# Scores of a second-half attention head issued as one run over three PSUM banks, and half of the weight splits placed later

## The chip, the cores and the metric

The kernel runs on one core of one Trainium2 chip. The metric is the device time of one execution in microseconds (us), of which the median over several runs is taken. The engines are named as in the profile: PE does matmuls (PEld is its weight load), DVE, ACT and POOL are the three engines for elementwise work, and SP issues the DMAs.

## The reference, cut to what matters

Attention with a causal mask and a decay, over 4 batches, 8 heads, 576 positions and 64 columns, is followed by a mixture of four experts over all 2304 tokens:

```python
scores = scale * q @ k.T                      # scale = 1/8
cum    = cumsum(log(clip(f, 1e-4, 1)))
scores = where(causal, -1e9, scores + cum[:, None] - cum[None, :])
attn   = exp(scores - max(scores)); attn /= sum(attn) + 1e-9
x      = attn @ v                             # heads side by side: 2304 x 512
p      = domain_probs / (sum(domain_probs) + 1e-9)
out    = sum over e of p[:, e] * (relu(x @ w1[e]) @ w2[e])   # 512 -> 1024 -> 512
```

## The kernel before, in words

**Attention.** The 576 queries of a batch are cut into a first half (queries 0 to 255) and a second half (256 to 575). A job is a batch, a pair of heads and a half, and its two heads are worked off one after the other, so there are 64 heads in `heads`: 0 to 31 of the first half, 32 to 63 of the second. This document names them by that number. A second-half head has three query tiles, t = 2, 3 and 4, with 384, 512 and 576 keys. For each tile PE makes the scores by pairs of matmuls (`s<-hi` and `s<-kl,q` in the profile, line 615): the first with the high parts of q and k, the second with the low parts and the decays. DVE adds the mask and takes the row minimum (`qk_min`, line 629), ACT takes the exponential and its sum (`qk_exp`, line 644). When a head's three tiles are through, `recip16` and `turn16` split the scaled probabilities in two f16 parts (ACT line 713, DVE line 714) and SP transposes them by DMA (`pt<-z`, line 723). `av_pair` (line 816) multiplies the transposed probabilities of both heads of a job with v, in 28 matmuls, and `out16` (line 870) writes the result into x.

**Inputs of the scores.** `prep_hi` and `prep_lo` make the operands of a head: ACT casts `hi<-raw` (line 562), POOL casts `q<-raw` (line 563) and takes two differences (`kl`, line 571, and `hi`, line 577). There are two buffers for `raw` and `hi` and one `q2` tile for each of the two heads of a job, so those of head n + 2 wait until the scores of head n have been made. The probabilities `p` have six buffers, three for a head.

**Banks.** Scores, transposes, `av_pair` and the small products of `power` take banks from the pool `ps_a`, which has four. `qk_pe` takes a new bank whenever a piece doesn't fit in the last one. A tile with 576 keys is made as two pieces of 288, and called tile by tile (`qk_tile`) the four pieces of a head take four banks: one each for t = 2 and 3, two for t = 4.

**Experts.** A `Step` is one pair of weight units (256 of the 1024 hidden columns of an expert) for one chunk of 256 tokens: `l1` (24 matmuls, line 1012), `gate` (ACT line 1025 makes `gh`, DVE line 1026 makes `gl`), `l2` (12 matmuls, line 1045), and after every second one DVE adds to `acc` (line 1072). There are 80 steps in two sweeps. Sweep 0 takes steps 0 to 27. In sweep 1 (steps 28 to 79) a group of four units is used for 4, 3 or 2 chunks, so for 8, 6 or 4 steps, alternating between its first pair (ps = 0) and its second (ps = 1). The last four chunks (`LAST`) are done by 16 larger products afterwards (`Big`, line 1283, from about 625 us).

**Weights.** `w_split(n)` splits unit n into two f16 parts by three engines: ACT lines 979 and 974, DVE line 980, POOL lines 971 and 975. It also has SP load up to three further units (`w_load`, line 937; three buffers) and two steps later write the split unit to DRAM (line 988). After the last step of a pair (`ends`) the pair six units further on is split. As the two pairs of a group end in neighbouring steps, four units are split in two neighbouring steps.

**The order.** Outside `startup` the program order is a priority, and the framework's scheduler puts each engine's instructions in order by that priority and by its own estimate of when their inputs are ready. The program order comes from a list: `head_steps` gives every piece of a head with a cost, and `pace(n)` emits, between the quarters of step n, as many pieces as the costs allow at an even slope between goals. A goal is that the x of a chunk is complete three steps before the step which first uses it. For chunk 4 that is step 40. When the x of chunk c is complete, three pieces find its scale (`turn`: L260, L199, L202 to L252) and `narrow(c)` makes `y` from it (ACT line 475, DVE line 476), which line 1012 reads. `narrow` is asked for once at the start of each step.

## Time and profile before

| | us |
|---|---|
| median of 3 runs | 942.64 |
| lowest and highest | 941.62, 944.03 |
| the profiled execution | 939.25 |
| its span, first to last instruction | 937.5 |

| stretch of the profiled execution, us | what runs there |
|---|---|
| 0 to 245 | first-half heads, steps 0 to 27 |
| 245 to 357 | second-half heads 33 to 44, steps 28 to 39 |
| 357 to 600 | heads 45 to 63, steps 40 to 75 |
| 600 to 937.5 | last steps, then the larger products |

The profile is one execution, 3.4 us under the median. The first view to read is the busy time by stretch with the granted clock of PE (1.00 is 2.4 GHz, and the lower of the two levels is 0.5), then what PE waited for in a stretch, then the timeline of the stretch. A line of the timeline gives start, duration, engine, source line, operation, output and inputs, and in brackets how long the engine had been idle and what ended that.

### The profile page before, as it was taken

The page shows a single profiled execution, that of the slowest core. Times are in us where ns is not written, and L with a number is a line of the kernel's source. Part 1 is how long each engine was busy: PE and PEld are TensorE (multiplying, and loading weights), DVE is VectorE, ACT ScalarE, POOL GpSimd, SP SyncE. Part 2 cuts the span into 40 slices and gives each one's busy share as a digit, 9 for nine tenths or more (in the row PEclk, how much of TensorE's full clock was granted, in tenths as well). Part 3 has the DMA queues.
Part 4 walks back from the last instruction along what each step waited for, and adds up shares of the span by engine and source line. Part 5 has one row for each costly group of instructions (what it writes and reads, how often), then busy time and mean ns, then how long its engine had stood idle before and what let it go on. Part 6 is the DMA issues. An engine that isn't in the chain of part 4 may idle for free. (4 is left out here: it accounts for less than half of the span.)

```text
span 937.5 us, 16657 instructions
## 1 busy us (share of the span) xinstructions
PE 885.3 (94%) x5783; PEld 620.8 (66%) x5783; DVE 709.3 (76%) x1458; ACT 568.9 (61%) x1137; POOL 525.1 (56%) x528
## 2 busy tenths in 40 slices
PE   4899998999998889999999989999998999999998
PEld 3699988999765556666666656654455664666547
DVE  5768665786888988789878887576778757786487
ACT  5869755465676778668666777355665345653350
POOL 4657865478533754327641684265778627785060
PEclk9999999999998988999999999999999999999999
DMA  7458844538879698988999699524322424232003
GB/s 264 146 176 295 291 126 164 186 119 313 227 189 198 152 293 195 311 156 212 306 288 158 119 328 236 135 67 142 129 91 81 145 68 125 79 107 74 23 1 91
DMA packets 147508, 159.45 MB, mean 170 GB/s; under 512 B 86148, under 2 KB 107328, under 8 KB 147424
## 3 DMA queue, kind: packets, MB, share of 16 engines
q1 hardware_dynamic: 147424, 158.39, 60.2%
q8 instruction: 45, 0.74, 0.3%
q14 instruction: 39, 0.32, 0.2%
HBM read 117.30 MB, written 21.65 MB: 148 GB/s over the span
## 5 line engine op out<-in xcount | busy, mean ns | idle before, releaser
L1012 PE MATMUL l<-y,w 128*128 128x256 f16 x1248 | 155.7, 275 | 0.0
L1012 PEld LDWEIGHTS <-w 128*128 128x128 f16 x1248 | 118.3, 99 | 30.6 <-issue 6.5
L644 ACT ACTIVATE p<-p,nm 128x576 f32<-128x576 f32 (+3 forms) x160 | 95.6, 598 | 52.4 <-DVE nm L629 43.5
L1045 PE MATMUL l<-w,gh 128*128 128x512 f16 x408 | 122.6, 383 | 4.8 <-DVE acc L1072 4.8
L714 DVE SCALAR_TENSOR_TENSOR z<-p,rs,z 128x384 f16<-128x384 f32 (+3 forms) x128 | 85.7, 694 | 12.6 <-ACT z L713 11.1
L1072 DVE SCALAR_TENSOR_TENSOR acc<-y,scg,acc 128x256 f32<-128x256 f32 (+1 forms) x164 | 81.1, 515 | 14.9 <-PE y L1283 14.7
L615 PE MATMUL s<-hi 128*128 128x384 f32 (+1 forms) x192 | 76.9, 406 | 16.1 <-DVE hi L577 8.9
L563 POOL CAST q<-raw 64x320 fp32r<-64x320 f32 (+1 forms) x56 | 26.0, 465 | 117.9 <-PE s L615 71.3
L1283 PE MATMUL m<-rh,bs 128*128 128x512 f16 x256 | 86.4, 379 | 0.0
L629 DVE CUSTOM_DVE_ANT_0 p<-s,mask 128x288 f32<-128x288 f32 (+2 forms) x160 | 74.8, 475 | 12.9 <-PE s L615 11.8
L571 POOL TENSOR_TENSOR kl<-raw,hi 64x576 fp32r<-64x576 f32 (+1 forms) x56 | 66.4, 1186 | 28.6 <-ACT hi L562 28.2
L1045 PE MATMUL l<-w,gl 128*128 128x512 f16 x204 | 77.1, 383 | 5.0 <-DVE gl L1026 5.0
L1209 POOL TENSOR_TENSOR bs<-wt,bs 128x512 f16<-128x512 f32 x32 | 38.4, 1201 | 75.7 <-ACT bs L1208 75.4
L971 POOL TENSOR_SCALAR wr<-wr,wsc 128x512 f32<-128x512 f32 x32 | 53.9, 1687 | 35.1 <-DMA wr<-in_w 25.5
L956 POOL TENSOR_TENSOR wl<-wr,wh 128x512 fp32r<-128x512 f32 x48 | 64.4, 1370 | 15.9 <-ACT wh L952 11.6
L713 ACT ACTIVATE z<-p,rs 128x384 f16<-128x384 f32 (+3 forms) x128 | 69.5, 589 | 4.6 <-issue 1.2
L1026 DVE SCALAR_TENSOR_TENSOR gl<-l,gh 128x512 f16<-128x512 f32 (+1 forms) x80 | 54.7, 684 | 19.1 <-ACT gh L1025 18.6
L1012 PE MATMUL l<-xh,wh 128*128 128x256 f32 x224 | 65.0, 292 | 0.8 <-ACT xh L857 0.8
L615 PE MATMUL s<-kl,q 66*128 66x384 f32 (+1 forms) x192 | 63.7, 336 | 2.2 <-DMA kl<-nc 2.2
L1283 PE MATMUL m<-rh,bw 128*128 128x512 f16 x191 | 64.4, 379 | 1.4 <-ACT r L1329 1.4
L1012 PE MATMUL l<-xl,wh 128*128 128x256 f32 x224 | 65.2, 291 | 0.0
L1045 PEld LDWEIGHTS <-gh 128*128 128x128 f16 x408 | 37.0, 98 | 42.2 <-issue 11.2
(387 smaller groups left out, 2359.6 us busy)
## 6 DMA issues: line engine op xcount, KB each, us to landing
wr<-in_w SPq DMA_DIRECT2D x90, 512.0 KB
pk<-in_w SPq DMA_DIRECT2D x64, 256.0 KB
wd<-w SPq DMA_DIRECT2D x32, 512.0 KB
raw<-in_qk SPq DMA_DIRECT2D x32, 448.0 KB
bw<-wd SPq DMA_DIRECT2D x32, 256.0 KB
bv<-wd SPq DMA_DIRECT2D x32, 256.0 KB
raw<-in_qk SPq DMA_DIRECT2D x24, 256.0 KB
vp<-in_v SPq DMA_DIRECT2D x10, 512.0 KB
```

Of the source, the lines that this page charges most:

```text
L571: eng.tensor_tensor(out=kl[:64, :wk], in0=r[:64, ko : ko + wk], in1=hi[:64, ko : ko + wk].bitcast(F32), op=ALU.subtract,)
L615: nc.tensor.matmul(out=ps[:, at : at + z - a], lhsT=lhsT, rhs=rhs, start=(m == 0), stop=(m == 1),)
L629: nc.vector.tensor_tensor_reduce(out=pt[:, a:z], in0=ps, in1=mask[:, m0 + a : m0 + z], scale=-0.125, scalar=BIG if n == 0 else nm[:, col : ...
L644: nc.scalar.activation(out=pt[:, :w_], in_=pt[:, :w_], func=AF.Exp, scale=-1.0, bias=self.nmax[hh][:, c : c + 1], accum_out=self.ssum[:, h ...
L713: nc.scalar.activation(out=o[:, 0], in_=x, func=AF.Copy, scale=sc)
L714: nc.vector.scalar_tensor_tensor(out=o[:, 1], in0=x, scalar=sc, in1=o[:, 0], op0=ALU.mult, op1=ALU.subtract)
L956: eng.tensor_tensor(out=wl[n][:, a:z], in0=r[:, a:z], in1=wh[n][:, a:z].bitcast(F32), op=ALU.subtract,)
L1012: nc.tensor.matmul(out=self.l1p[:, fi, :], lhsT=lhsT, rhs=rhs[:, k, :], start=(k == 0 and m == 0), stop=(k == 3 and m == 2),)
L1026: self.last = nc.vector.scalar_tensor_tensor(out=self.gl, in0=self.l1p, scalar=0.0, in1=self.gh.bitcast(F32) if wide else self.gh, op0=ALU ...
L1045: matmul(out=l2[tt], lhsT=lhsT, rhs=rhs, start=(self.ps == 0 and fi == 0 and m == 0), stop=(self.ps == 1 and fi == 1 and m == 2),)
L1072: nc.vector.scalar_tensor_tensor(out=acc[c][:, tt, d0:d1], in0=ps, scalar=sc, in1=acc[c][:, tt, d0:d1], op0=ALU.mult, op1=ALU.add,)
L1283: line.append(nc.tensor.matmul(**args))
```

## The change

`qk_head` makes all scores of a second-half head in one call, over three banks taken together. Tile 2 lies in 384 columns of the first bank and tile 3 fills the second. Tile 4 is cut at key 448 instead of 288: its last 128 keys go into the 128 free columns of the first bank, its first 448 into the third. `qk_pe` loses the cut, since only first-half heads still call it. In the list, `qk_head` stands first with cost 1400, and then each tile's `qk_min` and `qk_exp` with cost 224. The sum is that of the three old costs (584 + 712 + 776 = 2072). `av_pair` of the job before, when there is one, stands after the third entry instead of the second, so after `qk_min` and `qk_exp` of tile 3.

`REST` postpones those calls of `w_split` that follow the end of a group's second pair, by 1, 2 or 3 steps where the group is used for 2, 3 or 4 chunks.

```diff
+REST = (0, 0, 1, 2, 3)
...
+        def qk_bank(self, hh, t):
+            return ps_a.tile([128, 512], F32, tag="a", name=f"s{self.nm}_{hh}_{t}")
+
+        def qk_piece(self, hh, t, a, z, ps):
+
+            o, i = self.qo + TOK0[t] - self.q0, TOK0[t] - self.q0
+            for m, (lhsT, rhs) in enumerate(
+                (
+                    (self.hi[hh][:, o : o + 128], self.hi[hh][:, self.ko + a : self.ko + z]),
+                    (q2[hh][:, i : i + 128], self.kl[hh][:66, a:z]),
+                )
+            ):
+                nc.tensor.matmul(out=ps, lhsT=lhsT, rhs=rhs, start=(m == 0), stop=(m == 1))
+            self.sp.setdefault((hh, t), []).append((a, z, ps))
...
-                cuts = ((0, w_),) if w_ <= 512 else ((0, w_ // 2), (w_ // 2, w_))
...
+                if at + w_ > 512:
+                    ps, at = self.qk_bank(hh, t), 0
+                self.qk_piece(hh, t, 0, w_, ps[:, at : at + w_])
+                at += w_
+
+        def qk_head(self, hh):
+
+            two, three, four = (self.qk_bank(hh, t) for t in (2, 3, 4))
+            self.qk_piece(hh, 2, 0, 384, two[:, :384])
+            self.qk_piece(hh, 4, 448, 576, two[:, 384:])
+            self.qk_piece(hh, 3, 0, 512, three)
+            self.qk_piece(hh, 4, 0, 448, four[:, :448])
...
+            if j.half:
+                qs.append((1400, lambda j=j, hh=hh: j.qk_head(hh)))
             for t in j.its:
-                qs.append((TOK0[t] + 328, lambda j=j, hh=hh, t=t: j.qk_tile(hh, t)))
+                if j.half:
+                    qs.append((224, lambda j=j, hh=hh, t=t: (j.qk_min(hh, t), j.qk_exp(hh, t))))
+                else:
+                    qs.append((TOK0[t] + 328, lambda j=j, hh=hh, t=t: j.qk_tile(hh, t)))
...
-            qs[2:2] = [(1000, j.av_pair), (0, j.out16)] + ready(n - 2)
+            qs[3:3] = [(1000, j.av_pair), (0, j.out16)] + ready(n - 2)
...
-                        w_split(w0 + 6)
-                        w_split(w0 + 7)
+                        wait = REST[len(SWEEPS[t.s][t.g // 2])] if t.ps else 0
+                        splits.setdefault(n + wait, []).extend((w0 + 6, w0 + 7))
                     first_units(w0)
+            for m in splits.pop(n, ()):
+                w_split(m)
```

## Rows read from the trace of the kernel before

**Rows 1.** The page: PE's busy time, and all row minima (count, busy, mean).

```profile
PE 885.3 (94%) x5783; PEld 620.8 (66%) x5783; DVE 709.3 (76%) x1458; ACT 568.9 (61%) x1137; POOL 525.1 (56%) x528
...
L629 DVE CUSTOM_DVE_ANT_0 p<-s,mask 128x288 f32<-128x288 f32 (+2 forms) x160 | 74.8, 475 | 12.9 <-PE s L615 11.8
```

**Rows 2.** By stretch: PE, PEld, DVE, ACT, POOL busy (count); PEclk; DMA share; GB/s.

```profile
245.00:357.00 112.00, 99.18 (x651) 66.11 (x650) 98.76 (x231) 78.46 (x159) 56.50 (x54) 0.90 0.89 217
357.00:600.00 243.00, 236.36 (x1761) 161.98 (x1758) 198.34 (x432) 165.97 (x336) 114.14 (x104) 1.00 0.92 225
```

**Rows 3.** What PE waited for, 245 to 357: total, times, longest.

```profile
PE s L615 <- POOL hi L577: 4.8, 2, 2.5
PE o L816 <- DMA pt<-z: 4.0, 1, 4.0
PE l L1045 <- DVE acc L1072: 2.5, 2, 1.9
PE l L1045 <- DVE gl L1026: 1.4, 2, 1.0
```

**Rows 4.** The timeline of PE around the scores of head 37.

```profile
288.89 0.44 PE L816 MATMUL o<-pt,v 128*64 128x320 f16 x1 [3.98 <-DMA pt<-z]
...
292.44 2.35 PE L816 MATMUL o<-pt,v 128*64 128x320 f16 x27
294.72 0.40 PE L615 MATMUL s<-hi 128*128 128x288 f32 x1
```

**Rows 5.** The timelines of DVE, ACT and POOL at the same place.

```profile
291.03 0.46 DVE L629 CUSTOM_DVE_ANT_0 p<-s,mask 128x288 f32<-128x288 f32 x1 [1.06 <-PE s L615]
...
295.30 0.52 DVE L629 CUSTOM_DVE_ANT_0 p<-s,mask,nm 128x288 f32<-128x288 f32 x1 [2.15 <-PE s L615]
...
296.12 0.94 ACT L562 ACTIVATE hi<-raw 128x896 fp32r<-128x896 f32 x1
...
295.39 0.45 POOL L563 CAST q<-raw 64x320 fp32r<-64x320 f32 x1 [10.17 <-DMA raw<-in_qk]
```

**Rows 6.** What DVE waited for, 245 to 357, the first line.

```profile
DVE p L629 <- PE s L615: 3.6, 4, 2.1
```

**Rows 7.** The timeline: `av_pair` of head 39, `y` of chunk 4, first matmul of step 40.

```profile
332.63 1.72 PE L816 MATMUL o<-pt,v 128*64 128x320 f16 x27
...
350.93 1.98 DVE L476 SCALAR_TENSOR_TENSOR y<-xf,xsc,y 128x1024 f16<-128x1024 f32 x1 [0.64 <-ACT y L475]
...
356.42 0.39 PE L1012 MATMUL l<-y,w 128*128 128x256 f16 x1
```

**Rows 8.** The timeline of PE: starts of score matmuls of 128, 288 and 512 columns.

```profile
221.40 0.28 PE L615 MATMUL s<-hi 128*128 128x128 f32 x1
221.51 0.28 PE L615 MATMUL s<-kl,q 66*128 66x128 f32 x1
...
302.06 0.40 PE L615 MATMUL s<-hi 128*128 128x512 f32 x1
302.30 0.40 PE L615 MATMUL s<-kl,q 66*128 66x512 f32 x1
...
423.75 0.29 PE L615 MATMUL s<-hi 128*128 128x288 f32 x1
423.88 0.30 PE L615 MATMUL s<-kl,q 66*128 66x288 f32 x1
```

**Rows 9.** What PE waited for, 357 to 600: total, times, longest.

```profile
PE l L1045 <- DVE gl L1026: 3.6, 3, 2.1
PE l L1045 <- DVE acc L1072: 1.7, 2, 1.3
PE o L816 <- DMA pt<-z: 1.3, 2, 1.0
```

**Rows 10.** The timeline: a split that waits for its raw unit, and PE after it.

```profile
541.22 0.72 ACT L979 ACTIVATE w<-wr,wsc 128x512 f16<-128x512 f32 x1 [4.58 <-DMA wr<-in_w]
...
543.44 0.59 PE L1045 MATMUL l<-w,gh 128*128 128x512 f16 x2 [1.32 <-DVE acc L1072]
```

More of the change, by code (lines that the diff above doesn't have):

```diff
@@ L600, in qk_pe @@
             for t in its:
-                o = self.qo + TOK0[t] - self.q0
                 w_ = TOK0[t] + 128
-                cuts = ((0, w_),) if w_ <= 512 else ((0, w_ // 2), (w_ // 2, w_))
-                for n, (a, z) in enumerate(cuts):
-                    if at + z - a > 512:
-                        ps = ps_a.tile([128, 512], F32, tag="a", name=f"s{self.nm}_{hh}_{t}_{n}")
-                        at = 0
-                    i = TOK0[t] - self.q0
-                    for m, (lhsT, rhs) in enumerate(
-                        (
-                            (self.hi[hh][:, o : o + 128], self.hi[hh][:, self.ko + a : self.ko + z]),
-                            (q2[hh][:, i : i + 128], self.kl[hh][:66, a:z]),
-                        )
-                    ):
-                        nc.tensor.matmul(
-                            out=ps[:, at : at + z - a],
-                            lhsT=lhsT,
-                            rhs=rhs,
-                            start=(m == 0),
-                            stop=(m == 1),
-                        )
-                    self.sp.setdefault((hh, t), []).append((a, z, ps[:, at : at + z - a]))
-                    at += z - a
+                if at + w_ > 512:
[8 more added lines that the diff above has]
+            self.qk_piece(hh, 4, 0, 448, four[:, :448])
         def qk_min(self, hh, t):
@@ L1618, in fused @@
         w_split(n)
-    used = set()
+    used, splits = set(), {}
     for n in range(len(steps) + 1):
```

## The prediction

> **What bounds the kernel now.** The page comes first: PE is busy for 885.3 of 937.5 us [rows 1], so at most the idle remainder and what a lower clock costs can be won without removing matmuls. The change removes none. The view by stretch shows where the remainder lies that the change can reach, since second-half heads run from 235 to 600 us only. From 357 to 600 us PE is busy for 236.4 of 243.0 us at full clock, which leaves 6.6 us. From 245 to 357 us it is busy for 99.2 of 112.0 us, and its mean granted clock is 0.90 [rows 2]. With levels of 1.0 and 0.5, a mean of 0.90 says that a fifth of the stretch, some 22 us, ran at the lower level, and half of that, 11 us, is time that the same matmuls would not have taken at the upper one. So this stretch holds 12.8 us of idle time and up to 11 us of slow matmuls, and it is the one to understand.
>
> Its end is not set by PE. Step 40 is the first to use chunk 4. The `av_pair` that completes this chunk's x (head 39) runs at 332.6 us, the last part of `y` is written from 350.9 to 352.9 us, and step 40 begins at 356.4 us [rows 7]. Step 39 had begun before 340, so PE had only attention left to do, and waited twice for its operands (4.8 us for POOL's `hi`, [rows 3]). The chain to this `y` runs through heads 33 to 39, whose work on DVE queues behind each other: DVE is busy for 98.8 of 112.0 us [rows 2]. So the stretch can shorten only by as much as DVE's 13.2 us of idle time allow.
>
> One place shows how the idle time arises. Behind tile 3 of head 37 stands, on PE, the `av_pair` of head 35, which waits 4.0 us for its transposes, until 288.9; the rest of it runs at 292.4, and the last two pieces of head 37 come at about 290 and at 294.7 [rows 4]. DVE, which needs them for its minima, sits idle for 1.06 and 2.15 us [rows 5], and these two are 3.2 of the 3.6 us that it waits for scores in the whole stretch [rows 6]. ACT's `hi` for head 39, which needs the buffer of head 37, comes at 296.1, directly after. Its raw data came hardly sooner, as POOL's cast of the same head waited for them until 295.4 [rows 5], so the buffer was not the only thing it lacked. Head 39 is the one that completes chunk 4.
>
> **The change part by part.**
>
> *Place of the scores.* I worked out the planner's positions by hand from the costs. Head 37 had tiles 2 and 3 at steps 29.25 and 29.75, `av_pair` of head 35 at 30.375, and tile 4 at 30.875. Now all scores stand at 29.625, the minima at 29.75 and 29.875, `av_pair` at 30.5, and the minimum of tile 4 at 30.625. Twelve heads lie in the stretch and all odd ones have this pattern. No score then stands behind an `av_pair` of the same section, so the 3.6 us of DVE waits go. `hi` and `q` of head n + 2 get their buffers earlier, and the `av_pair` stands half a step further from the `turn16` it needs (for head 37: 30.625 to 33.75 instead of 30.875 to 33.5), which is some 3 us (steps 40 to 75 take 243 us [rows 2], 6.7 us a step with the attention in it). DVE's idle time is what the chain to `y` can use, so I credit the 3.6 us to the end of the stretch. After `y` was ready, PE needed until 356.4, 3.5 us, for attention matmuls at the lower clock [rows 2, 7]. When there are fewer stalls ahead of it, part of this goes too: I take 2.0 us. Together −5.6 us. The bounds are 0 (DVE fills its idle time with something else) and −13.2 us (all of it is used).
>
> *Minima in one place.* The cost of the four minima of a head does not change: 0.475 us each [rows 1], 1.9 us a head, 128 + 448 columns being as many as 288 + 288. But three entries now stand 0.125 step apart, so up to 1.9 us of DVE work come together where single ones (at most two pieces) came before. Queued behind it on DVE are `gl`, which `l2` of PE waits for, and `acc`. In the stretch that PE sets (357 to 600, 19 heads) there are three stalls on `gl` of 1.2 us on average [rows 9]. I add one more, +1.2 us. The bounds are 0 and seven more, +8.4 us.
>
> *Pieces of 128 and 448.* Matmuls of 288 columns start 0.13 us apart, those of 512 columns 0.24, and those of 128 columns 0.11 [rows 8]. By the line between 288 and 512, one of 448 takes 0.21. A head had 4 × 0.13 = 0.52 for tile 4 and gets 2 × 0.11 + 2 × 0.21 = 0.64. That is +0.12 us a head, paid where PE is the bound: 19 × 0.12 = +2.3 us. The bounds are 0, if the short ones stream in proportion to their columns (0.06 us), and +3.7 us for 31 heads.
> The Trainium skill, "TensorE: Matmul & The Clock Gate", section "Back-to-back issue gap", speaks against this cut as well: it gives about 81 ns for a sustained matmul of 128 columns, well above the 56 ns of an isolated one, as the weight load has to fit in. By its figures the two cuts differ by an estimated 0.05 us a head, or 1 us in place of 2.3; the row is above the Trainium skill's figure.
>
> *Three banks at once.* The pool has four. A run needs three free ones, which are those of the head before after its last minimum, and `av_pair` takes the fourth. I cost this at nothing: PE's list of waits has no wait for `nm`, the minimum that frees a bank, in either stretch [rows 3, 9]. If that cover goes, while `power` holds a bank for chunk 4, the scores of head 42 wait for it, which is attention ahead of its need.
>
> *Chunk 4's scale.* The pieces of `turn` move from step 36.75 to 37.0, and `narrow` is therefore asked for at step 38 instead of 37. I cost this at nothing, as the chain runs 18 us behind its x by data (334.3 to 352.9), not by its place in the program [rows 7]. If it were set by place, it would cost the quarter step to one step, 1.7 to 6.7 us.
>
> *Splits.* The pairs that move are units 24, 28 and 32, 36, 44, 48, 52, 56 and 60 with their neighbours, by 1 to 3 steps. With each go its two casts on ACT, one instruction on DVE, two on POOL, and on SP the loads of the units behind it and two writes to DRAM, which then stand behind the transposes of later heads. The three raw buffers are what makes the fourth unit of a burst wait: ACT stands 4.6 us for a raw unit, and PE then waits 1.3 us for the `acc` queued behind on DVE [rows 10]. With two units at a time the raw data are there, −1.3 us; the bounds are 0 and −1.7 us, all waits for `acc` there [rows 9]. In the other direction, a pair that was split early may now fall into the tight stretch. It brings two instructions to DVE and four to ACT, and the later place of units 36 and 37 (28.99 to 30.99) lies in it. I take nothing for it, as it is far from the step that needs them.
>
> *Transposes later on.* The extra half step should also end the waits for `pt<-z` after 357: −1.3 us [rows 9], between 0 and that.
>
> **Sum.** −5.6 + 1.2 + 2.3 − 1.3 − 1.3 = −4.7 us. The profiled execution took 939.25 us, its span and 1.75 us around it, and would take 934.5. The median of the runs shown lies 3.4 us above the profiled execution; the same difference from the median of 942.64 gives 937.9 us, 0.5% faster.
>
> **The rivals.**
>
> *DVE stays the bound, or the run is not made.* The program order is only a priority. The scheduler may still spread the pieces over the PE queue, and where it does make the run, DVE may fill its gaps with peeks and splits so that `y` comes when it came before. For it speaks that DVE is busy 88% of the stretch and that the work ahead of chunk 4 is the same. Against it speaks that the idle time has the scores' name on it [rows 5, 6]. The first term falls away, and +1.2 + 2.3 − 1.3 − 1.3 leaves +0.9: 943.5 us.
>
> *Minima before `gl`: slower.* If the block of minima falls ahead of `gl` in a third of the 19 heads, seven stalls of 1.2 us come on top. `l2` of a step stands behind the `l1` of the next, and that one `l1` is all the slack that the gate has; a block of 1.9 us directly ahead of `gl` uses up most of it. For it speaks that DVE is busy for 198 of 243 us there [rows 2]. Against it speaks that the scheduler puts `gl` where it expects it ready. 8.4 + 2.3 − 2.6 = +8.1 us without the first term, 950.7; with half of it (−2.8), 947.9. It turns into a loss from the fifth such stall on.
>
> *The whole idle time is used.* If the heads move up as a whole and PE stays at its upper clock, the first term is −13.2: 930.3 us. The 4.0 us at 288.9 and the 4.8 us for `hi` would both vanish.
>
> **How the numbers follow.** About 0.3% is what a measurement of this kernel can tell from no change: faster means under 939.8, slower over 945.5. I give the forecast 0.42, all the idle time 0.10, no net effect 0.28 and the block of minima 0.20. The predicted time is the forecast's, 938 us. Its own range is 934 to 942. Both signs hold a good part, so the range reaches from 931 to 947.5, leaving out the extremes of the two outer cases. Of the forecast a part (0.06) lies within 0.3%, of the case without effect 0.05 lies above: faster 0.46, same 0.29, slower 0.25.
>
> **What would show it.** The first step is right if PE's queue shows eight score matmuls of a head in a row and DVE's waits for scores between 245 and 357 are near 0. The second is right if step 40 begins before 353 us and the stretch's clock is above 0.90. A longer list of waits for `gl` after 357 would show the third. The short pieces are right at 0.11 us from start to start. The forecast is wrong if step 40 begins no earlier although DVE doesn't wait for scores any more: then the chain to `y` was never bound by them.

## The result and the profile after

The change made the kernel slower: 952.17 us against 942.13 us (medians of four runs each, from 950.67 to 956.23 and from 937.15 to 944.03), a ratio of 1.0127 with a 95% interval from 1.0104 to 1.0149. The prediction was 938 us, in a range from 931 to 947.5. The profiled execution of after took 950.67 us and has a span of 948.9 us; that of before has a span of 937.5.

In after all line numbers lie higher: scores 610 (before 615), minima 635 (629), exponential 650 (644), ACT's and DVE's part of z 719 and 720 (713 and 714), `av_pair` 822 (816), `l1` 1023 (1012), `gh` 1036 (1025), `gl` 1037 (1026), `l2` 1056 (1045), `acc` 1083 (1072).

The page of after, first the busy times (they answer to [rows 1]), then DVE's part of z (group, count, busy, mean ns, idle before):

```profile
PE 886.1 (93%) x5783; PEld 621.4 (65%) x5783; DVE 721.9 (76%) x1458; ACT 568.0 (60%) x1137; POOL 524.6 (55%) x528
...
L720 DVE SCALAR_TENSOR_TENSOR z<-p,rs,z 128x384 f16<-128x384 f32 (+3 forms) x128 | 92.5, 750 | 14.4 <-ACT z L719 12.1
```

The same group in before:

```profile
L714 DVE SCALAR_TENSOR_TENSOR z<-p,rs,z 128x384 f16<-128x384 f32 (+3 forms) x128 | 85.7, 694 | 12.6 <-ACT z L713 11.1
```

PE does the same work in 0.8 us more and is idle for 62.8 us (948.9 − 886.1) where it was idle for 52.2: nearly all of the loss is idle time of PE. DVE, with the same 1458 instructions, is busy for 12.6 us more, 6.8 of it in the 128 instructions that write z's low half and 4.9 in the 32 that write the weights' low half (28.4 us before, 33.3 after).

By stretch (the columns of [rows 2]):

```profile
245.00:357.00 112.00, 96.93 (x646) 64.00 (x646) 101.19 (x236) 79.00 (x162) 54.56 (x53) 0.96 0.85 213
357.00:600.00 243.00, 230.22 (x1688) 158.89 (x1686) 198.71 (x420) 162.44 (x330) 113.80 (x104) 0.98 0.89 223
```

From 245 to 357 the mean granted clock rose from 0.90 to 0.96, as hoped, and PE's idle time rose with it, from 12.8 to 15.1 us. From 357 to 600 the idle time went from 6.6 to 12.8 us. What PE waited for, 245 to 357 (it answers to [rows 3]):

```profile
PE o L822 <- DMA pt<-z: 4.7, 4, 2.8
PE l L1056 <- DVE gl L1037: 3.7, 5, 1.4
PE s L610 <- DVE nm L635: 2.6, 2, 1.8
PE l L1056 <- DVE acc L1083: 1.4, 1, 1.4
PE o L822 <- DVE nm L635: 1.1, 1, 1.1
PE l L1056 <- ACT gh L1036: 0.7, 1, 0.7
PE l L1023 <- DVE y L477: 0.2, 1, 0.2
```

and 357 to 600 ([rows 9]):

```profile
PE l L1056 <- ACT gh L1036: 6.9, 2, 3.5
PE l L1056 <- DVE acc L1083: 3.1, 2, 1.9
PE o L822 <- DMA pt<-z: 2.7, 2, 1.7
```

POOL's `hi`, 4.8 us in before, is gone. In its place stand waits for banks (`nm`, 3.7 us, none in this trace of before) and, above all, longer waits of `l2` for the gate and for `acc`: 15.8 us in the two lists (3.7 + 1.4 + 0.7 + 6.9 + 3.1) against 9.2 (2.5 + 1.4 + 3.6 + 1.7). The costliest new name is ACT's `gh`, for which PE waited nowhere in the two stretches before.

The run of scores is made as the change says. PE around one head:

```profile
452.79 0.42 PE L610 MATMUL s<-hi 128*128 128x384 f32 x1
...
453.22 0.23 PE L610 MATMUL s<-hi 128*128 128x128 f32 x1
453.28 0.27 PE L610 MATMUL s<-kl,q 66*128 66x128 f32 x1
453.39 0.45 PE L610 MATMUL s<-hi 128*128 128x512 f32 x1
...
453.92 0.37 PE L610 MATMUL s<-hi 128*128 128x448 f32 x1
454.12 0.37 PE L610 MATMUL s<-kl,q 66*128 66x448 f32 x1
454.34 0.83 PE L1023 MATMUL l<-y,w 128*128 128x256 f16 x6
```

Eight score matmuls stand in a row, in 1.55 us from the first start to the next `l1`. DVE's list of waits from 245 to 357 holds no wait for scores any more (3.6 us before, [rows 6]). And step 40 begins no earlier ([rows 7]: 356.42):

```profile
358.91 0.58 PE L1023 MATMUL l<-y,w 128*128 128x256 f16 x2
```

What came in the way is the `y` of chunk 4, whose last part is done at 358.5 us, against 352.9 in before [rows 7]. Its x is complete later (the search for its largest value, `xmax`, ends on DVE at 341.0 us, against 337.3), and the small instructions that find its scale take longer. They go from PE (`topx`, L200) over four of DVE's (`ux`) back to PE (L221). In after:

```profile
341.04 0.27 PE L200 MATMUL topx<-ident,xmax 128*1 128x128 f32 x1
344.34 0.28 DVE L203 TENSOR_REDUCE ux<-topx 1x1 f32<-1x128 f32 x1
...
350.49 0.20 DVE L214 TENSOR_SCALAR ux<-ident,ux 1x1 f32<-1x1 f32 x1
351.40 0.38 PE L221 MATMUL topx<-ux,ones_r 1*128 1x1 f32 x2
...
357.17 1.29 DVE L477 SCALAR_TENSOR_TENSOR y<-xf,xsc,y 128x1024 f16<-128x1024 f32 x1
```

and in before:

```profile
338.42 0.27 PE L199 MATMUL topx<-ident,xmax 128*1 128x128 f32 x1
...
343.12 0.38 PE L220 MATMUL topx<-ux,ones_r 1*128 1x1 f32 x2
```

Between the two matmuls lie 10.4 us in after and 4.7 in before. In DVE's queue seven minima of two heads stand between the first and the last of the `ux` in after, and three in before. From the end of `xmax` to the end of `y` it is 17.5 us against 15.6.

One of the two long stalls on `gh`, on ACT and then on PE:

```profile
459.91 0.63 ACT L985 ACTIVATE w<-wr 128x512 f16<-128x512 f32 x1 [0.79 <-POOL wr L982]
460.45 0.60 ACT L650 ACTIVATE p<-p,nm 128x384 f32<-128x384 f32 x1
...
461.89 0.70 ACT L990 ACTIVATE w<-wr,wsc 128x512 f16<-128x512 f32 x1
462.50 0.70 ACT L650 ACTIVATE p<-p,nm 128x512 f32<-128x512 f32 x1
...
463.20 0.57 ACT L1036 ACTIVATE gh<-l 128x512 f16<-128x512 f32 x1
```

```profile
463.83 0.60 PE L1056 MATMUL l<-w,gh 128*128 128x512 f16 x2 [3.42 <-ACT gh L1036]
```

`gh` needs nothing but `l1`, which PE had finished at 460.4. On ACT it stands behind casts of weight units, one of which waits 0.79 us for POOL, behind a cast `hi` of 0.93 us, and behind two exponentials, which need DVE's minima. The scores of this head had been there since 454.5. The second stall, at 584.34, lies just ahead of the last stage:

```profile
576.26 1.42 POOL L1188 TENSOR_TENSOR wt<-wr 128x256 f32<-128x256 f32 x2 [8.20 <-DMA wr<-in_w]
```

```profile
579.20 1.33 ACT L1215 ACTIVATE wt<-wt,wsc 128x512 f32<-128x512 f32 x2 [4.59 <-POOL wt L1188]
...
583.71 0.58 ACT L1036 ACTIVATE gh<-l 128x512 f16<-128x512 f32 x1
```

```profile
584.34 0.81 PE L1056 MATMUL l<-w,gh 128*128 128x512 f16 x2 [3.48 <-ACT gh L1036]
```

Here POOL waited 8.20 us for raw weights of the last stage, ACT 4.59 us for POOL, and `gh` stood behind ACT's pieces of that stage.

### The profile page after: what moved, and what is told of

It is laid out like the page before. It is cut to its first block, busy times and chain, and to the rows that moved or that the text cites. A ratio compares the mean times of both kernels' runs of the same rounds, so it can differ in the third digit from the quotient of the medians.

```text
span 948.9 us, 16639 instructions
## 1 busy us (share of the span) xinstructions
PE 886.1 (93%) x5783; PEld 621.4 (65%) x5783; DVE 721.9 (76%) x1458; ACT 568.0 (60%) x1137; POOL 524.6 (55%) x528
## 5 line engine op out<-in xcount | busy, mean ns | idle before, releaser
L1023 PE MATMUL l<-y,w 128*128 128x256 f16 x1248 | 150.7, 273 | 0.2 <-DVE y L477 0.2
L720 DVE SCALAR_TENSOR_TENSOR z<-p,rs,z 128x384 f16<-128x384 f32 (+3 forms) x128 | 92.5, 750 | 14.4 <-ACT z L719 12.1
L610 PE MATMUL s<-hi 128*128 128x384 f32 (+1 forms) x192 | 69.8, 372 | 14.2 <-DVE hi L578 8.7
L719 ACT ACTIVATE z<-p,rs 128x384 f16<-128x384 f32 (+3 forms) x128 | 69.6, 590 | 14.8 <-issue 6.8
L635 DVE CUSTOM_DVE_ANT_0 p<-s,mask 128x128 f32<-128x128 f32 (+1 forms) x160 | 66.9, 443 | 11.3 <-PE s L610 10.0
L967 POOL TENSOR_TENSOR wl<-wr,wh 128x512 fp32r<-128x512 f32 x48 | 64.7, 1373 | 14.8 <-ACT wh L963 8.6
```

The costliest lines, as they stand in the source:

```text
L610: nc.tensor.matmul(out=ps, lhsT=lhsT, rhs=rhs, start=(m == 0), stop=(m == 1))
L635: nc.vector.tensor_tensor_reduce(out=pt[:, a:z], in0=ps, in1=mask[:, m0 + a : m0 + z], scale=-0.125, scalar=BIG if n == 0 else nm[:, col : ...
L719: nc.scalar.activation(out=o[:, 0], in_=x, func=AF.Copy, scale=sc)
L720: nc.vector.scalar_tensor_tensor(out=o[:, 1], in0=x, scalar=sc, in1=o[:, 0], op0=ALU.mult, op1=ALU.subtract)
L967: eng.tensor_tensor(out=wl[n][:, a:z], in0=r[:, a:z], in1=wh[n][:, a:z].bitcast(F32), op=ALU.subtract,)
L1023: nc.tensor.matmul(out=self.l1p[:, fi, :], lhsT=lhsT, rhs=rhs[:, k, :], start=(k == 0 and m == 0), stop=(k == 3 and m == 2),)
```

## The experiments

Ratios are to the kernel before, run beside each on the same chip, with the 95% interval.

### Each part alone

**Only the later splits** (the last hunk of the change, on the kernel before):

```diff
+                        wait = REST[len(SWEEPS[t.s][t.g // 2])] if t.ps else 0
+                        splits.setdefault(n + wait, []).extend((w0 + 6, w0 + 7))
...
                     first_units(w0)
+            for m in splits.pop(n, ()):
+                w_split(m)
```

> The kernel before with REST alone: the second pairs of weight units are split 1 to 3 steps later, the scores are made tile by tile as before. The changed kernel took 952.2 us against 942.1 (+1.1%), and in its profile PE waits 6.9 us for ACT's gh in two places, 460.4 to 463.8 and 580.9 to 584.3 us, where ACT had stood behind casts of weight units that waited for raw units or for POOL's sums. Theory A (the splits make the loss): this run shows both stalls and takes 949 to 955 us. Theory B (the run of scores and its block of minima make it): no stall for gh over 2 us in these places, 939 to 945 us. Theory C (each part costs a bit): 945 to 949 us.

948.54 us, ratio 1.0088 (1.0048 to 1.0128). **Only the run** (everything but that hunk):

> The changed kernel without REST: scores of a second-half head in one run over three banks, splits where they were before. Theory A: the stalls behind the casts go and the time is that of the kernel before or less, 936 to 945 us, with step 40 beginning no later than 356.4 us. Theory B: 949 to 955 us, with the stalls spread over many places between 245 and 600 us. Theory C: 945 to 949 us.

950.07 us, ratio 1.0114 (1.0087 to 1.0140). **The whole change, but units 60 and 61 split at their old place**, ahead of `first_units(54)`:

```diff
+                        if w0 in EARLY:
+                            w_split(w0 + 6)
+                            w_split(w0 + 7)
+                        else:
+                            splits.setdefault(n + wait, []).extend((w0 + 6, w0 + 7))
                     first_units(w0)
```

> The changed kernel, but of the moved pairs the last one (units 60 and 61) keeps its old place ahead of the first sums for the larger products (first_units). In the changed kernel these sums came first in the program, so their raw units take a buffer before units 60 and 61 have given theirs back, POOL waits 8.2 us for them and ACT 4.6 us, with gh behind. Theory A in its narrow form (the second stall is made by this pair's order): the wait for gh at 581 to 584 us goes, and the time falls by 4 to 8 us against the changed kernel, to 944 to 948 us. If that stall has another cause, 950 to 954 us.

950.0 us, ratio 1.0105 (1.0085 to 1.0124). So each part loses about 1% by itself, and together they lose hardly more. No one of the three theories had foreseen both. The trace of the splits alone has no wait for `gh` from 245 to 640 us, against theory A. In the third kernel the wait for `gh` at 584 us is down to 0.3 us, as the narrow form of theory A had it, but the time fell by some 2 us and not by 4 to 8. The two losses are of different kinds, as the traces show: with the splits alone, the `l2` of every step up to 73 ends within 2.7 us of its time in before, and then one wait of 5.1 us for a transpose follows during the `l1` of step 75. With the run alone the delay builds up in many small waits, 8.6 us between the ends of steps 27 and 79.

### The splits

**The pair of units 60 and 61 taken out of the later splits.**

```diff
-                        wait = REST[len(SWEEPS[t.s][t.g // 2])] if t.ps else 0
+                        wait = REST[len(SWEEPS[t.s][t.g // 2])] if t.ps and w0 != 54 else 0
                         splits.setdefault(n + wait, []).extend((w0 + 6, w0 + 7))
```

> Only the later splits, on the kernel before, without the pair that precedes the first units of the last stage (units 60 and 61), which stay where they were. Theory L (all of the loss of the later splits is that pair: SyncE's issues get in another order, the transposes of the last pair of heads are late and av_pair waits 5.1 us for them at 594): no such wait, and 938 to 942. Theory S (any later split loses): 946 to 950.

948.22 us, ratio 1.0058 (1.0036 to 1.0080), with a wait of 5.83 us at the same place. My edit didn't do what its expectation says: the pair now stands in the same step as before, but still behind `first_units`, since the later splits are emitted there. Compared instruction by instruction, the built kernel has the order of the one with the later splits alone on every engine. POOL and PE in it:

```profile
566.41 1.86 POOL L1178 TENSOR_TENSOR wt<-wr 128x256 f32<-128x256 f32 x2 [7.17 <-DMA wr<-in_w]
...
569.34 1.41 POOL L572 TENSOR_TENSOR kl<-raw,hi 64x576 fp32r<-64x576 f32 x1
```

```profile
602.29 3.16 PE L817 MATMUL o<-pt,v 128*64 128x320 f16 x27 [5.83 <-DMA pt<-z]
```

POOL waits 7.17 us for a raw weight of the last stage (line 1178), and the difference `kl` of the last head stands behind it. In before, that difference stood ahead of it:

```profile
563.82 1.40 POOL L571 TENSOR_TENSOR kl<-raw,hi 64x576 fp32r<-64x576 f32 x1
...
568.80 1.41 POOL L1177 TENSOR_TENSOR wt<-wr 128x256 f32<-128x256 f32 x2 [2.64 <-issue]
```

The last head's scores, its z and its transposes are late by that, and `av_pair` waits.

**The pair ahead of the first units in the program as well.**

```diff
+                        if wait:
+                            splits.setdefault(n + wait, []).extend((w0 + 6, w0 + 7))
+                        else:
+                            w_split(w0 + 6)
+                            w_split(w0 + 7)
```

> Later splits on the kernel before, units 60 and 61 kept ahead of the first units of the last stage in the program. The build puts every instruction but three issues of SyncE in the order of before, so theory L (only that pair behind the first units loses) expects the time of before, 938 to 944, and no wait of 5 us for a transpose at 594. Theory S (any later split loses): 946 to 950.

941.57 us, ratio 0.9991 (0.9968 to 1.0015). All the other pairs were still asked for 1 to 3 steps later, and the built order is that of before but for a few issues of SP. So the whole loss of the later splits is the pair of units 60 and 61 behind `first_units`. The other moves do nothing, as the scheduler built the same order for them. (That it goes by the time at which a raw buffer comes free is my guess.) The trace of this kernel is thus a second execution of before's order, and it shows how far one trace may differ from the next: PE waits 3.3 us for `nm` and 1.0 us for transposes in the two stretches from 245 to 600 us, where the trace of before has none and 5.3, and the granted clock from 245 to 357 is 0.94 and not 0.90.

### The run: its place, its minima, its pieces

**The run at the place of the first tile, minima at the costs of before.**

```diff
             for t in j.its:
+                if j.half:
+                    qs.append((TOK0[t] + 328, lambda j=j, hh=hh, t=t: (
+                        t == 2 and j.qk_head(hh), j.qk_min(hh, t), j.qk_exp(hh, t))))
...
+            qs[2:2] = [(1000, j.av_pair), (0, j.out16)] + ready(n - 2)
```

> The run of eight score matmuls where before had the first tile's scores, each tile's minima and exponential at the costs that they had before (584, 712, 776, av_pair after the second), splits in the order of before. Theory M (the minima in a block, and what they do to the narrowing of p and the gate values behind them, make the loss): with the minima back 939 to 943.5, VectorE's narrowing (z) back near 89 us in all. Theory R (the run itself: eight matmuls at one go that cost 0.10 us more per head, and three of four banks taken at once): 947 to 952, z near 89 us or not, TensorE waiting for minima of scores (bank waits) 3 us or more.

945.76 us, ratio 1.0025 (1.0005 to 1.0044). **Scores tile by tile as before, the minima of tiles 2 and 3 late.**

```diff
+                qs.append((584, lambda j=j, hh=hh: j.qk_pe(hh, (2,))))
+                qs.append((712, lambda j=j, hh=hh: j.qk_pe(hh, (3,))))
+                qs.append((328, lambda half=half: half(2)))
+                qs.append((224, lambda half=half: half(3)))
+                qs.append((224, lambda j=j, hh=hh: j.qk_tile(hh, 4)))
```

> Scores of each tile by themselves, in the pieces and at the places of before; the minima and exponentials of the first two tiles put off by 1040 and 552 of the planner's cost, to where the change has them. Theory M: 946 to 952, z 96 to 100 us against 89. Theory R: 938 to 943.5.

942.59 us, ratio 0.9999 (0.9979 to 1.0019). Neither theory holds for both. Late minima alone cost nothing, the early run alone little, and both together 1%.

**Only the cut of the last tile.**

```diff
-                cuts = ((0, w_),) if w_ <= 512 else ((0, w_ // 2), (w_ // 2, w_))
+                cuts = ((0, w_),) if w_ <= 512 else ((0, w_ - 448), (w_ - 448, w_))
```

> The kernel before with the last tile's scores cut 128 + 448 instead of 288 + 288, each tile still by itself. If the pieces' 0.10 us per head lies on the path: 0.10 x 32 = 3 us, 943 to 948. If TensorE's idle time takes it up: 938 to 943.

943.48 us, ratio 1.0005 (0.9987 to 1.0024). Where the four matmuls of the last tile stand in a row on PE, they take 0.82 us here from the first start to the next instruction's, and 0.68 in before (medians of 25 and 24 heads), so 32 heads would pay some 4.4 us, an estimate. The time shows at most 2.3 us of it (0.0024 × 942). The idle time takes up the rest.

**The preparation of the next head behind the run.**

```diff
-            st.append((0, lambda j=j, hh=hh: j.prep(hh)))
+            if not heads[n][0].half:
+                st.append((0, lambda j=j, hh=hh: j.prep(hh)))
...
+            qs[1:1] = [(0, lambda j=j, hh=hh: j.prep(hh))]
```

> The run with its minima in a block (splits in the order of before), and the preparation of the next head (GpSimd's two subtractions above all) put behind the run of scores and no longer at the head of the step list, right behind the previous head's z. Theory Z (z takes 1.2 to 1.8 us instead of 0.58 where a subtraction of GpSimd runs beside it, which happens more often with the block: z 99.6 us in all against 88.8, and that is the loss): z 90 to 93 us and 941 to 945. Theory R or M without Z: z shorter or not, the time 948 to 952 as the run by itself.

949.46 us, ratio 1.0071 (1.0051 to 1.0091). It tests nothing of theory Z: the built order is, on all five engines, that of the run alone. It is therefore a second measurement of that kernel. With the kernel of units 60 and 61 at their old place, in which only two instructions of a split and a few issues of SP stand elsewhere, there are three, and the run loses 0.7 to 1.1%, 9 us in the mean.

### DVE beside GpSimd

What the kernels with the run have in common is seen best at one head. POOL, DVE and PE with the run alone:

```profile
440.42 1.16 POOL L986 TENSOR_TENSOR w<-wr,w 128x512 f16<-128x512 f32 x1
442.66 1.16 POOL L986 TENSOR_TENSOR w<-wr,w 128x512 f16<-128x512 f32 x1 [1.08 <-ACT w L985]
443.76 0.91 POOL L564 CAST q<-raw 64x320 fp32r<-64x320 f32 x1
444.65 1.15 POOL L986 TENSOR_TENSOR w<-wr,w 128x512 f16<-128x512 f32 x1
```

```profile
440.73 5.16 DVE L720 SCALAR_TENSOR_TENSOR z<-p,rs,z 128x384 f16<-128x384 f32 x4
445.91 0.56 DVE L635 CUSTOM_DVE_ANT_0 p<-s,mask 128x384 f32<-128x384 f32 x1
...
447.22 0.69 DVE L1037 SCALAR_TENSOR_TENSOR gl<-l,gh 128x512 f16<-128x512 f32 x1
...
448.42 0.74 DVE L1083 SCALAR_TENSOR_TENSOR acc<-l,scg,acc 128x512 f32<-128x512 f32 x1
```

```profile
449.21 0.59 PE L1056 MATMUL l<-w,gh 128*128 128x512 f16 x2 [1.87 <-DVE acc L1083]
```

The four narrowings of z take 5.16 us here. Behind them come three minima of the next head's run, then `gl` and `acc`, and PE waits 1.87 us for `acc`. In before the four narrowings at this place took 3.25 us, with `acc` between them, and PE did not wait:

```profile
440.81 1.22 DVE L714 SCALAR_TENSOR_TENSOR z<-p,rs,z 128x384 f16<-128x384 f32 x1
441.96 0.74 DVE L1072 SCALAR_TENSOR_TENSOR acc<-l,scg,acc 128x512 f32<-128x512 f32 x1
442.62 2.03 DVE L714 SCALAR_TENSOR_TENSOR z<-p,rs,z 128x512 f16<-128x512 f32 x3
```

Over all 128 narrowings of after, one takes 0.59 us on average where POOL does nothing (73 of them), 0.75 beside POOL's one-source work (26) and 1.16, at most 1.78, beside a two-source subtraction (29). `gl` and `acc`, which read PSUM and one tile of SBUF, took the same beside POOL and alone: in after a `gl` took 0.684 us beside a two-source subtraction (36 of them) and 0.685 where POOL does nothing (33), and 234 `acc` took 136.5 us in before and in after (sum of their durations). The Trainium skill, "SBUF — State Buffer", section "Who interferes with whom", says that a DVE instruction with two SBUF inputs contends with a GpSimd instruction that reads SBUF, and that one with at most one such input, outside the 2-port perf modes, does not contend with GpSimd. The trace agrees on both halves, with the figures of the two sentences before. A DVE instruction with one source in SBUF can be held up too: `ss` (line 678 in after, and 666), on 3 or 4 columns, took 0.16 us where POOL does nothing (17) and 0.62 beside a subtraction (27); whether it runs in such a mode no run here shows.

The expectations give z by the sum of its durations, 88.8 us in before and 99.6 with the run alone. The lists of groups count overlapping pieces once and give 85.7 and 96.0, which the text uses.

**One-source copies for GpSimd's subtractions**, on the run and on the kernel before. The low parts of k, q and half the columns of the weights are left out (the high value stands in their place):

```diff
-            eng.tensor_tensor(
-                out=kl[:64, :wk],
...
+                nc.gpsimd.tensor_copy(out=kl[:64, :wk], in_=r[:64, ko : ko + wk])
+                nc.gpsimd.tensor_copy(out=hi[64:128, qo : qo + wq], in_=r[64:128, qo : qo + wq])
...
-                    nc.gpsimd.tensor_tensor(
-                        out=wl[n][:, c], in0=r[:, c], in1=wh[n][:, c], op=ALU.subtract
-                    )
+                    nc.gpsimd.tensor_copy(out=wl[n][:, c], in_=r[:, c])
```

> The run (splits in the order of before) with GpSimd's two-source subtractions in the second half's head preparation and in the weight splits replaced by one-source copies: the low parts are left out (the high value stands in their place). To be read against the same on the kernel before. Theory Z (VectorE's narrowing takes 1.2 to 1.8 us for 0.58 where such a subtraction runs beside it, and gate values and sums queue behind it; the run lets it happen more often): z near 80 us in both kernels, and the run loses 2 to 4.5 us only, which its two added pieces cost (0.10 us for each of 32 heads). Theory K (three banks taken at once and the minima in a block make the loss, whatever GpSimd does): the run loses 7 to 11 us here too, with TensorE's waits for gate values as long as in the run by itself.

> The kernel before with the same copies for subtractions (low parts left out). Theory Z: z near 80 us (88.8 before), 933 to 941. Theory K: z may be shorter, the time within 3 us of before.

With the run 935.24 us, ratio 0.9899 (0.9868 to 0.9930); without it 935.34 us, 0.9911 (0.9877 to 0.9945). The run costs nothing that shows here (−0.1 us, interval about −5 to 3), and theory K with its 7 to 11 us falls: three banks at once and minima in a block don't lose that much by themselves. z went to 80.9 and 82.1 us in the lists of groups (84.5 and 85.4 as sums, not quite the 80 that was expected). But a copy is also shorter than a subtraction and doesn't wait for ACT's `hi`.

**A short narrowing**, 16 of each 128 (or 64) columns; the rest of z's low half stays zero:

```diff
-                    out=o[:, 1], in0=x, scalar=sc, in1=o[:, 0], op0=ALU.mult, op1=ALU.subtract
+                    out=o[:, 1, :, :16], in0=x[:, :, :16], scalar=sc,
+                    in1=o[:, 0, :, :16], op0=ALU.mult, op1=ALU.subtract,
```

> The run (splits in the order of before) with VectorE's narrowing of p cut to 16 of each 128 (or 64) columns: the rest of z's low half stays zero, a part of the low products is left out. GpSimd's subtractions are as they were. To be read against the same on the kernel before. Theory Z by way of VectorE (gate values and sums late because the narrowing before them in VectorE's queue is held up by GpSimd): the run loses 0 to 4 us, as with the copies. If the loss goes by way of GpSimd itself (its subtractions late, and the scores behind them): the run still loses 6 to 10 us.

> The kernel before with the same short narrowing. VectorE has some 60 us less to do; if it set the pace of the stretches 245 to 357 and 357 to 600 by its narrowing, 930 to 937; if not, 938 to 943.

With the run 930.0 us, 0.9887 (0.9856 to 0.9917); without it 925.72 us, 0.9837 (0.9795 to 0.9879). The kernel without the run gained more than was expected (930 to 937). Step 40 began at 342.40 and 340.56 us, 14 to 16 us sooner than in before, so DVE's narrowing lies on the way to the first `y` of chunk 4. The run still loses 4.3 us, just above the 0 to 4 of theory Z, and the interval of that difference reaches from about 0 to 10. A short narrowing isn't short beside a subtraction: 0.92 us with the run, on average of the eleven that met only the subtraction of a weight split, and 0.75 of all 24 that met any, against 0.26 with POOL idle.

**Fills in place of subtractions.** A subtraction of 16 columns keeps the wait for ACT, two fills with zero that only write keep the time; the low parts beyond 16 columns are left out:

```diff
+                    nc.gpsimd.tensor_tensor(
+                        out=wl[n][:, a], in0=r[:, a], in1=wh[n][:, a], op=ALU.subtract
+                    )
+                    for _ in range(2):
+                        nc.gpsimd.memset(wl[n][:, 512 * k + 16 : 512 * k + 512], 0.0)
```

(and the same for `kl` and `hi`)

> The run (splits in the order of before) with each of GpSimd's two-source subtractions in the second half's head preparation and in the weight splits replaced by a subtraction of 16 columns, which keeps the wait for ScalarE, and two fills with zero of all the others, which only write and together take about as long (1.16 us for 512 columns). The low parts beyond 16 columns are left out. To be read against the same on the kernel before. Lock theory (a narrowing of VectorE with both sources in SBUF stands still while GpSimd reads SBUF): z 78 to 86 us in all, and the run loses 0 to 4 us. Late operands (GpSimd's time and waits): z the same or not, the run loses 6 to 10 us.

> The kernel before with the same fills for subtractions. Lock theory: z 78 to 84 us against 88.8, 932 to 941. Late operands: 938 to 944.

With the run 935.25 us, 0.9937 (0.9909 to 0.9964); without it 930.26 us, 0.9887 (0.9842 to 0.9931). The group of z, with the run and without:

```profile
L732 DVE SCALAR_TENSOR_TENSOR z<-p,rs,z 128x384 f16<-128x384 f32 (+3 forms) x128 | 75.7, 617 | 9.6 <-ACT z L731 8.3
```

```profile
L726 DVE SCALAR_TENSOR_TENSOR z<-p,rs,z 128x384 f16<-128x384 f32 (+3 forms) x128 | 77.0, 628 | 9.0 <-ACT z L725 7.8
```

GpSimd is nearly as long at work as before (517.1 us, 525.1 before), and most of its reading in these places is gone. Beside fills alone a narrowing takes 0.55 us with the run (16 of them) and 0.63 without (18), as it does with POOL idle (0.61 and 0.59). The narrowing falls from 85.7 to 77.0 us, and the kernel before gains 11 us, more than the lock theory's 932 to 941 us had it. I put this down to the meeting of the two engines: the change only adds to a loss that is there without it. The run costs 5.0 us here (interval about 0 to 10), at the middle between the two theories: 9 us as it is, and −0.1, 4.3 and 5.0 us where DVE's time or the meeting is taken away, 3.1 in the mean. So some 6 of the 9 us go with the meeting, as an estimate from differences that are each uncertain by about 5.

What the other 3 us are isn't shown. They are not PE's time for the scores. The run has eight matmuls a head, as many as before, and with PE's idle time taken out they take 1.70 us in after and 1.82 in before, where they are made tile by tile (means of 32 heads, from start to start).

What PE waits for `gh`, `gl` and `acc` from 245 to 640 us in each profiled execution, all such waits added up:

| kernel | ratio | gate and acc, us | z busy, us |
|---|---|---|---|
| before | | 9.8 | 85.7 |
| splits, last pair ahead | 0.9991 | 8.3 | 86.0 |
| splits alone, and the same order again | 1.0088, 1.0058 | 9.1, 9.3 | 86.8, 86.8 |
| late minima, no run | 0.9999 | 10.3 | 87.2 |
| pieces only | 1.0005 | 9.3 | 89.6 |
| run, old minima | 1.0025 | 13.9 | 95.3 |
| run alone, and the same order again | 1.0114, 1.0071 | 14.4, 16.2 | 96.0, 94.8 |
| run, later splits, last pair at its old place | 1.0105 | 16.4 | 98.4 |
| after | 1.0127 | 15.9 | 92.5 |
| copies: before, run | 0.9911, 0.9899 | 4.6, 6.3 | 82.1, 80.9 |
| short z: before, run | 0.9837, 0.9887 | 3.0, 7.5 | 40.5, 44.1 |
| fills: before, run | 0.9887, 0.9937 | 1.0, 4.4 | 77.0, 75.7 |

Every kernel with the run has 3.4 us or more of such waits on top of its partner without it, except with the copies (1.7). More time on DVE alone doesn't do it: in the kernel with the pieces only, z takes 3.9 us more and DVE is busy for 720.7 us (709.3 before, 721.9 after), and it has no more waits and no loss that shows (its trace is of an execution of 946.05 us, its median 943.48). Nor do the waits rank the times. The run with the old minima has nearly the waits and the z of the run alone and loses a quarter as much; but its trace is that of the slowest of its ten executions (948.98 us, median 945.76), and that of the run alone of the fastest of four (947.05, median 950.07).

## Why the prediction was wrong, point by point

**The credit for the stretch to step 40 (−5.6 us) is the step that failed.** DVE's waits for scores went from 3.6 us to none, as foreseen. The prediction named the sign that would refute the credit, step 40 beginning no earlier although those waits are gone, and it came: 358.91 against 356.42. The other traces bear it out. In the five with the run and all of DVE's work step 40 begins at 358.4 to 361.6 us, in the six without the run at 354.4 to 359.6; `y` of chunk 4 is done at 358.5 to 363.4 and at 351.7 to 356.2. So the waits for scores did not bind the chain to `y`. DVE's work does: less narrowing moved step 40 to 340.56 in the kernel without the run, and fills on POOL moved it to 342.62. DVE's idle time, which was to carry the gain, didn't turn into one; DVE was busy for 101.2 us there, 98.8 in before [rows 2] and 100.7 in the second execution of before's order. The 2.0 us for the time after `y` were there (0.5 us from the end of `y` to step 40, 3.5 in before), and the clock was higher (0.96; 0.90 in before, 0.92 to 0.94 in the other five without the run), but `y` came 5.6 us later. Why x of chunk 4 was complete 3.6 us later was not traced further.

**The minima (+1.2, bounds 0 and +8.4) were mis-sized, and the wait sits on another engine too.** The waits for gate values and `acc` rose by 6.6 us (9.2 to 15.8 in the two stretches), within the bound and near its upper end. The prediction looked at DVE's queue alone: `gl` behind the block of minima, with a longer list of waits for `gl` after 357 as the sign. After 357 that list is empty (3.6 us before). In after PE waits 7.6 us for ACT's `gh`, which needs no minimum but stands in ACT's queue behind exponentials that need one and behind weight casts. And the minima were costed as a block of 1.9 us; the block that held `acc` up at 448.42 in the run alone began with 5.16 us of narrowing.

**What it had not seen at all** is that an instruction of DVE can take twice its time because of what POOL does beside it. The row existed: in the trace of before, 28 narrowings beside a two-source subtraction took 0.86 us on average and up to 1.89, against 0.61 alone. I had taken "the cost of the four minima does not change" as if the same were true of everything on DVE.

**The pieces (+2.3) were costed for matmuls at an even pace.** The new cut was given 0.64 us. In the run it takes 0.59: the two of 128 columns start 0.06 and 0.11 us apart from the next (453.22 to 453.39 above), those of 448 columns 0.21 as predicted (453.92 to 454.34). The old cut was given 0.52 and takes 0.68 in before, in the median of the 24 heads where it stands in a row, as the first of its matmuls, behind other work, takes 0.27 and not 0.13. So on PE the run saves a little and loses nothing (1.70 against 1.82 us a head). The cut costs only where tiles are made one by one, and there the time moved by 0.05%.

**The banks (nothing).** PE waited 3.7 us from 245 to 357 for minima that free a bank, 2.6 us for scores and 1.1 us for `av_pair`, where the trace of before has no such wait. But the second execution of before's order has 3.3 us of them, so they are not shown to be the run's. The cover, one trace without such a wait, was too thin to rest a zero on.

**The splits (−1.3) failed for another reason than weighed.** I had moved them by the program's place. Only the pair of units 60 and 61 changed its place in the built order, behind `first_units`, and that alone made the 0.6 to 0.9% of the kernels with the later splits only. With the run the same pair cost some 2 us (952.17 against 950.0, each beside its own runs of before: 1.0127 against 1.0105), a difference within the intervals; the stall of 3.48 us at 584.34 is its place in the trace.

**The transposes (−1.3).** PE's waits for them went from 5.3 us [rows 3, 9] to 7.4 in the two stretches. The credit isn't seen; but the second execution of before's order has 1.0, so the term was as large as the difference between two executions.

**Chunk 4's scale (nothing) failed as well.** The prediction held that the chain runs by data and not by its place. In after it runs by its place in DVE's queue: its small instructions stand between the minima of two heads, and the chain from x to `y` takes 17.5 us against 15.6. In the other four traces with the run it takes 18.2 to 21.3, in the others without it 14.8 to 16.1, so the run makes it 3.6 us longer in the mean. PE's wait of 0.2 us for `y` doesn't show this, as PE spends the time on attention or waits for transposes.

**The rivals.** "Minima before `gl`: slower" (0.20, 947.9 to 950.7) came nearest. Its place was right, its account of what fills DVE's queue was incomplete, and the splits' last pair was not in it. My argument against it, that the scheduler puts `gl` where it expects it ready, doesn't hold at a place like 447.22, behind narrowings that took 5.16 us where the trace of before has 3.25.

**What stays open.** Why the late minima and the run lose only together was not settled: the rows of one head show the narrowing, the block and `gl` in one queue, but no kernel varied their order by itself. Nor is it shown why the pieces-only kernel bears as much DVE time as after without a loss. The remaining 3 us of the run without the meeting of DVE and POOL could be its place in the queues or nothing; the intervals don't tell.

## What to carry to other kernels

When an edit moves work in time, list for every engine what stands in its queue between the moved work and the next operand that the bound engine waits for, ACT's exponentials as well as DVE's minima. Look in the trace for instructions of one kind whose durations differ, and for what runs beside the long ones: work that is moved may meet it more often. A place in the program is no place in the queue; compare the built order before giving a moved step a price. A wait read from one trace is one execution: two executions of one order (but for a few issues of SP) differed here by 3.3 us in the waits for banks and by 4.3 in those for transposes, so a credit of 1 or 2 us on such a row needs a second trace.

## What the runs showed of the hardware that I had not expected

A DVE instruction with both sources in SBUF can wait for GpSimd's instruction beside it whatever its own length: narrowings cut to an eighth or a quarter of their columns fell from 0.58 to 0.26 us alone (with the run), but took 0.92 us beside the subtraction of a weight split (eleven of them). When GpSimd only writes, this goes: with fills of the same length the narrowing fell to 77.0 us, the low half of the weights on DVE from 28.6 to 24.4 us (sums), and the kernel gained 1.1%.
